# A graph tensor product on one core: the edges in four parts instead of three, and the sums' product with its operands exchanged

## The chip, the cores and the metric

The kernel runs on one core of a Trainium2 chip. The core has five engines with queues of their own: TensorE for matmuls (PE in the profile; PEld is its loading of weights), VectorE (DVE), ScalarE (ACT), GpSimd (POOL) and SyncE (SP), which here only issues transfers (DMAs). The metric is the device time of one execution in microseconds. Each engine works through its own queue in order; semaphores tie the queues together.

## The reference

The graph has N = 10000 nodes and E = 640000 edges with random ends. A node carries x of 64 channels by 4 components, an edge carries Y of 4 values and 4 features.

```python
R = _silu(edge_feat @ w_rad)                              # (E, C)
xs = x[src]                                                 # (E, C, M)
tp = jnp.einsum('eci,ef,ifo->eco', xs, Y, cg)             # (E, C, M)
msg = R[:, :, None] * tp
agg = _segment_sum(msg.reshape(-1, C * M), dst, N).reshape(N, C, M)
return jnp.einsum('ncm,cd->ndm', agg, w_mix)
```

All in float32. Since cg and w_mix don't depend on the edge, the kernel sums over edges first: for each node n it forms G[c, i, f] = sum over its edges of R[c] x[src][c, i] Y[f], 64 by 4 by 4 numbers, and multiplies that once by the product of w_mix and cg.

## The kernel before, in words

**Sorting by destination.** The sum over edges is a matmul with a one-hot matrix of destinations, so the edges have to lie together by destination. A bucket is 32 nodes (`NB`), 313 buckets in all; a group is 18 buckets (`B`), 18 groups, the last with 7 buckets. The edges, 128 to a column, make 5000 columns ("tiles"). They are cut into parts by `SPLIT`, each an entry of a share of the edges and the tiles that a bucket gets in this part, as a tuple of steps: `((0.26, (4,)), (0.47, (4, 4)), (0.27, (5,)))` is three parts, with one step of 4 tiles, two steps of 4, and one of 5. Together a bucket has 17 tiles (`BT`) of 128 places; what doesn't fit goes to an overflow area.

`pass1` sorts a part's edges into groups, `pass2` sorts a group of a part (a "segment") into buckets. Both work in chunks (12 and 11 tiles): places by small matmuls (`tables`, `places`), a one-hot matrix and the payload spread over rows (`spread`, DVE and ACT), a chain of matmuls that moves the rows (`move`, L560 and L562), an eviction on ACT (L567), and an indirect DMA on POOL that stores the rows in HBM (`store`, L571). `tables` (L319) is a chain of many small operations on PE, ACT and DVE, once for a block of pass 1 and once for a segment of pass 2; its first product is L333, its last L459. HBM areas for the rows of groups and of buckets are cleared first (`clear_groups`, L225; `clear_buckets`, L243).

**Messages.** `messages` walks the segments in order; a unit is one step of one bucket. For a unit, POOL gathers x of the sources (L785, one indirect DMA of 128 rows per tile), six units ahead, into eight buffers; PE transposes the payload (`turn`, L798), ACT copies it (L803), PE forms the radial product (`radial`, L808), ACT takes silu in place in PSUM (`silu`, L811), DVE multiplies x by it (`products`, L829) and builds S = onehot(dst) * Y, 128 columns of 32 nodes by 4 values, per tile (`spots`, L819 and L822). Then `sums` (L840) multiplies: for each tile and each half h of the 256 columns of V = R * x, V's half is the stationary operand and S streams past it, 128 moving columns:

```python
nc.tensor.matmul(G[:, h].rearrange("p n f -> p (n f)"),
                 V[:, t, 32 * h:32 * h + 32, :].rearrange("p c i -> p (c i)"),
                 S[:, t].rearrange("p n f -> p (n f)"), ...)
```

G lies in PSUM in one buffer, 128 channel-component rows of two halves by 128 columns. After the last step of a bucket in this part, `evict` takes it out: in the first part by an ACT copy (L871), later by a DVE add (L869) of the older sum, which `fetch` (L854) loads from HBM four units ahead. All but the last part store the sum in HBM again (`sums`, L873). In the last part the add writes Gs, four buckets side by side; `mix` (L888) multiplies Gs by the prepared weights with eight products of 256 moving columns, ACT copies the result (L896) and SP stores it.

**What sets the order.** The loop of `messages` runs over units, each in four quarters; the tuple `quarters` says which stage of which unit is emitted in which quarter (`(sums, 0)` the present unit, `(products, 1)` the next, `(gather, LG)` six on). PE, DVE and ACT run in the order in which this is written. `groups` puts steps of pass 2 of the next segment, and of pass 1 of the next part, between the quarters, evenly over the time there is. The first part's pass 1 has no messages beside it; only clearing is woven into it (`weave`). After the messages, `overflow` works through the rows that didn't fit, 128 edges in each trip of a loop.

Of the kernel before, what the change touches and what calls it, by code (L numbers as in the profile page):

```python
# [18 lines left out]
F = mybir.dt.float32  # L19
# [3 lines left out]
AF = mybir.ActivationFunctionType  # L23
AX = mybir.AxisListType

P = 128
B = 18
# [4 lines left out]
NB = 32  # L32
GN = B * NB
BT = 17
UT = 5
SPLIT = ((0.26, (4,)), (0.47, (4, 4)), (0.27, (5,)))
LG = 6
LI = 8
HEAVY = 4
# [32 lines left out]
class Kernel:  # L72
    def __init__(self, ctx, tc, x, src, dst, Y, ef, w_rad, cg, w_mix, out):
# [53 lines left out]
        self.p1.dst = self.dr.tile([self.p1.rows, self.p1.rw], F, name="grp")  # L127
        self.p2.dst = self.dr.tile([self.p2.rows, self.p2.rw], F, name="bkt")

        self.sums = self.dr.tile([self.NBK, P, 256], F, name="sums")  # L130
        self.in_group = {"grp": 0, "bkt": 0}
        self.tab = {}
        self.held, self.wanted, self.pos = None, False, None
# [607 lines left out]
    def messages(self):  # L741

        nc, ph = self.nc, self.ph
        units = [((k, g), j, s) for k, g in self.segs for j in range(self.nb(g)) for s in range(len(SPLIT[k][1]))]
        MT = max(sum(u) for _, u in SPLIT)
        n = len(units)
        IDX, XG, PRE, ST_, RT, SS, VS, GP, GS, OLD = ({} for _ in range(10))

        def quad(k):

# [80 lines left out]
        def sums(k):  # L831
            g, j, s = units[k]
            ut = tiles(k)[1]
            if s == 0:
                GP[g, j] = self.ps.tile([P, 2, NB, 4], F, name="G", tag="G", bufs=1)
            G = GP[g, j]
            V, S = VS.pop(k), SS.pop(k)
            for t in range(ut):
                for h in range(2):
                    nc.tensor.matmul(G[:, h].rearrange("p n f -> p (n f)"),  # L840
                                     V[:, t, 32 * h:32 * h + 32, :].rearrange("p c i -> p (c i)"),
                                     S[:, t].rearrange("p n f -> p (n f)"),
                                     start=(s + t + h == 0), stop=(last(k) and t == ut - 1),
                                     skip_group_check=True)

        def last(k):
            return units[k][2] == len(SPLIT[units[k][0][0]][1]) - 1

        def fetch(k):

            g, j, s = units[k]
            if g[0] and s == 0:
                OLD[g, j] = ph.tile([P, 2, 4, NB], F, name="old", bufs=4)
                nc.sync.dma_start(OLD[g, j].rearrange("p h f n -> p (h f n)"), self.sums[g[1] * B + j])  # L854

        def evict(k):
            g, j, s = units[k]
            if not last(k):
                return
            final = g[0] == len(SPLIT) - 1  # L860
            if not final:
                to = ph.tile([P, 2, 4, NB], F, name="Gp")
            else:
                if j % 4 == 0:
                    GS[g, j // 4] = ph.tile([P, 2, 4, 4, NB], F, name="Gs")
                to = GS[g, j // 4][:, :, :, j % 4, :]
            G = GP.pop((g, j)).rearrange("p h n f -> p h f n")
            if g[0]:
                nc.vector.tensor_tensor(to, OLD.pop((g, j)), G, op=OP.add)  # L869
            else:  # L870
                nc.scalar.activation(to, G, AF.Copy)  # L871
            if not final:
                nc.sync.dma_start(self.sums[g[1] * B + j], to.rearrange("p h f n -> p (h f n)"))  # L873

        def full(k):
            g, j, s = units[k]
# [15 lines left out]
        def mixed(k, po):  # L892
# [230 lines left out]
```

## Time and profile before

| | us |
|---|---|
| median of 3 runs | 10905.27 (10901.35 to 10920.43) |
| the profiled execution | 10989.96 |
| its span, first to last instruction | 10987.9 |
| first sums matmul (L840) starts | 726.6 |
| overflow loop and end, from | 10935 |

| engine | busy us | share | instructions |
|---|---|---|---|
| PE | 8420.1 | 77% | 52157 |
| PEld | 7126.3 | 65% | 52157 |
| DVE | 7056.8 | 64% | 13530 |
| ACT | 4102.8 | 37% | 12301 |
| POOL | 6003.7 | 55% | 6286 |

A float32 matmul stands as two records, each with its own weight load; a transpose is one. PE's busy time overlaps itself, since a record lasts longer than the distance to the next. In a row of a group, the numbers behind the bar are busy time, the mean of one in ns, and the idle time of the engine before these instructions with what ended it; "issue" is idle time for which no wait is seen. The mean granted clock of TensorE is 0.834. Units of the three parts begin at 727, 3678 and 8364 us.

### The profile page before, as it was taken

What the parts mean: (1) busy time and instruction counts of PE and PEld (TensorE: products, weight loads), DVE (VectorE), ACT (ScalarE), POOL (GpSimd) and SP (SyncE); (2) the same over time, 40 slices, a digit from 0 to 9 for tenths busy, and PEclk for the clock granted to TensorE, in tenths of its full rate; (3) what the DMA queues carried; (4) which work ended last, traced back from release to release, by engine and by line L of the source; (5) the groups of instructions that cost most, each with busy time, mean ns of one, the idle gap of its engine ahead of it and who ended that gap; (6) DMA issues with size and microseconds to landing.
All of it is one profiled execution on the core that took longest, in us unless ns stands there. A gap on an engine that the chain in (4) does not pass through costs nothing. (4 is left out here: it accounts for less than half of the span.)

```text
span 10987.9 us, 150963 instructions
## 1 busy us (share of the span) xinstructions
PE 8420.1 (77%) x52157; PEld 7126.3 (65%) x52157; DVE 7056.8 (64%) x13530; ACT 4102.8 (37%) x12301; POOL 6003.7 (55%) x6286
## 2 busy tenths in 40 slices
PE   6767787777877777777767777777767888888886
PEld 5656676666765666666656666666656666666665
DVE  7767777777766666666656666665546655656553
ACT  5645454554543433333333333333313222222220
POOL 1235455555555555555555556565566666666664
PEclk8878888888888888888888788888878888888887
DMA  7222222222223333333333333333333333333332
GB/s 155 77 62 80 83 84 86 83 82 85 87 84 93 96 99 98 99 98 99 99 94 97 92 95 102 98 103 97 96 110 103 106 107 107 104 104 107 107 103 86
DMA packets 695214, 1057.15 MB, mean 96 GB/s; under 512 B 251068, under 2 KB 499025, under 8 KB 694448
## 3 DMA queue, kind: packets, MB, share of 16 engines
q0 software_dynamic: 285872, 746.46, 23.6%
q1 hardware_dynamic: 405984, 294.29, 9.6%
q8 instruction: 413, 6.77, 0.3%
q10 hardware_dynamic: 2592, 6.74, 0.2%
q14 instruction: 353, 2.89, 0.1%
HBM read 856.14 MB, written 206.13 MB: 97 GB/s over the span
## 5 line engine op out<-in xcount | busy, mean ns | idle before, releaser
L785 POOL DMA_INDIRECT xg<-in_x_dram,sidx x5321 | 5052.2, 949 | 3344.1 <-issue 1371.8
L840 PE MATMUL G<-S,xg 128*128 128x128 f32 x21284 | 3250.8, 313 | 681.0 <-issue 395.4
L840 PEld LDWEIGHTS G<-S,xg 128*128 128x128 f32 x21284 | 3053.5, 226 | 797.3 <-issue 461.7
L560 PE MATMUL pr<-X,oh 128*128 128x126 f32 (+1 forms) x21252 | 3097.7, 306 | 604.6 <-ACT rt L567 294.1
L560 PEld LDWEIGHTS pr<-X,oh 128*128 128x128 f32 x21252 | 2929.4, 217 | 800.6 <-issue 384.2
L829 DVE TENSOR_TENSOR xg<-xg,pre 128x1024 f32<-128x1024 f32 (+1 forms) x1252 | 1603.8, 1281 | 866.8 <-ACT pre L811 705.8
L537 DVE TENSOR_TENSOR X<-dv,Wt 128x1485 f32<-128x1485 f32 (+3 forms) x941 | 1596.0, 1696 | 699.4 <-remote 413.2
L552 ACT ACTIVATE sq<-i,rowf 128x128 f32<-128x128 f32 x5640 | 1743.6, 393 | 5.6 <-DVE rowf L524 4.8
L811 ACT ACTIVATE pre<-pre 128x256 f32<-128x256 f32 (+1 forms) x1252 | 477.5, 381 | 2998.4 <-remote 990.0
L808 PE MATMUL pre<-wr,sT 36*128 36x256 f32 (+1 forms) x2504 | 1020.4, 490 | 310.1 <-ACT sT L803 256.4
L822 DVE TENSOR_TENSOR S<-dv,pay 128x512 f32<-128x512 f32 (+1 forms) x1252 | 907.6, 725 | 280.0 <-remote 131.0
L553 ACT ACTIVATE oh<-sq,ones 128x768 f32<-128x768 f32 (+1 forms) x941 | 928.5, 987 | 152.9 <-remote 50.9
L571 POOL DMA_INDIRECT grp<-rt,idx x417 | 415.2, 996 | 921.3 <-ACT rt L567 498.7
L571 POOL DMA_INDIRECT bkt<-rt,idx x524 | 524.8, 1002 | 646.6 <-ACT rt L567 422.0
L546 DVE TENSOR_TENSOR oh<-dv,rowf 128x768 f32<-128x768 f32 (+2 forms) x939 | 803.5, 856 | 0.3 <-PE pre L798 0.2
L808 PEld LDWEIGHTS pre<-wr,sT 36*128 36x128 f32 (+1 forms) x2504 | 414.6, 206 | 514.4 <-ACT sT L803 290.3
L567 ACT ACTIVATE rt<-pr 128x135 f32<-128x135 f32 (+1 forms) x941 | 253.6, 270 | 1075.9 <-remote 636.0
L869 DVE TENSOR_TENSOR Gs<-old,G 128x256 f32<-128x256 f32 x313 | 131.5, 420 | 766.5 <-PE G L840 277.9
L798 PE MATMUL pre<-ident,pay 128*36 128x128 f32 (+1 forms) x1252 | 383.2, 306 | 129.1 <-DVE xg L829 97.5
L798 PEld LDWEIGHTS pre<-ident,pay 128*36 128x36 f32 (+1 forms) x1252 | 132.7, 106 | 515.0 <-issue 235.5
L507 ACT ACTIVATE pc<-pp 128x432 f32<-128x432 f32 (+4 forms) x471 | 237.9, 505 | 559.7 <-remote 176.2
L803 ACT ACTIVATE sT<-pre 36x128 f32<-36x128 f32 (+1 forms) x1252 | 325.5, 260 | 285.6 <-PE pre L798 128.5
(214 smaller groups left out, 5164.6 us busy)
## 6 DMA issues: line engine op xcount, KB each, us to landing
xg<-in_x_dram,sidx POOLq DMA_INDIRECT x5321
sums<-Gp SPq DMA_DIRECT2D x626, 128.0 KB
old<-sums SPq DMA_DIRECT2D x626, 128.0 KB
bkt<-z SPq DMA_DIRECT2D x24, 994.5 KB
grp<-z SPq DMA_DIRECT2D x17, 679.5 KB
Wt<-grp SPq DMA_DIRECT2D x17, 679.5 KB
pay<-bkt SPq DMA_DIRECT2D x17, 648.0 KB
ys<-in_Y_dram SPq DMA_DIRECT2D x104, 96.0 KB
```

The lines of the kernel that those rows point to most:

```text
L537: nc.vector.tensor_tensor(X[:, :m, :].rearrange("p t (s w) -> p t s w", w=W), msk.unsqueeze(3).to_broadcast([P, m, ps.r, W]), QD[c // Q][1 ...
L546: nc.vector.tensor_tensor(oh[:, :v, :], self.v128.unsqueeze(1).to_broadcast([P, v, P]), row[:, o:o + v].unsqueeze(2).to_broadcast([P, v, P ...
L552: nc.scalar.activation(sq[:, u, :], self.i128, AF.Square, bias=to, scale=-1.0)
L553: nc.scalar.activation(oh[:, v:v + len(at), :], sq[:, :len(at), :], AF.Relu, bias=self.ones[:, 0:1], scale=-2.0)
L560: nc.tensor.matmul(pr[:, :ps.rw], oh[:, u, :], X[:, u, :], start=(u == 0), stop=(not on and u == m - 1))
L571: st = nc.gpsimd.indirect_dma_start(out=ps.dst, out_offset=bass.IndirectOffsetOnAxis(ap=idx[:, i:i + 1], axis=0), in_=RT.pop(c), in_offset ...
L785: nc.gpsimd.indirect_dma_start(out=xg[:, t, :], out_offset=None, in_=self.x, in_offset=bass.IndirectOffsetOnAxis(ap=si[:, u:u + 1], axis=0))
L798: nc.tensor.transpose(pre[:ut * W, 384:512], pb, self.ident)
L808: nc.tensor.matmul(R, ST_.pop(k)[:ut * W], self.wr[:ut * W, :ut * 64], start=True, stop=True)
L822: nc.vector.tensor_tensor(S[:, :ut], self.eq[:, :ut].unsqueeze(3).to_broadcast([P, ut, NB, 4]), pb[:, :, 1:5].unsqueeze(2).to_broadcast([P ...
L829: nc.vector.tensor_tensor(V, V, R.unsqueeze(3).to_broadcast([P, ut, 64, 4]), op=OP.mult)
L840: nc.tensor.matmul(G[:, h].rearrange("p n f -> p (n f)"), V[:, t, 32 * h:32 * h + 32, :].rearrange("p c i -> p (c i)"), S[:, t].rearrange( ...
```

## The change

There are four parts of one step each, with 3, 4, 5 and 5 tiles of a bucket; a bucket still has 17 tiles. In `sums`, S is the stationary operand and V streams past it with all its 256 columns, one matmul per tile; G then has the 128 node-value pairs as rows and the 256 channel-component pairs as columns. G and its transposed form take turns in the two halves of one PSUM bank. The sums in HBM keep their size, in the new orientation. In the last part the added sum stays in SBUF, two transposes per bucket (`flip`, a step later, behind the next unit's sums) bring it to the old orientation in the other half, and an ACT copy (`flipped`) writes it to Gs.

```diff
-SPLIT = ((0.26, (4,)), (0.47, (4, 4)), (0.27, (5,)))
+SPLIT = ((0.185, (3,)), (0.235, (4,)), (0.3, (5,)), (0.28, (5,)))
...
-        self.sums = self.dr.tile([self.NBK, P, 256], F, name="sums")
+        self.sums = self.dr.tile([self.NBK, NB * 4, 256], F, name="sums")
...
+        bank = self.ps.tile([P, 2, 256], F, name="G", tag="G", bufs=1)
+        turns = itertools.cycle((0, 1))
+        half = lambda: bank[:, next(turns), :]
...
-                GP[g, j] = self.ps.tile([P, 2, NB, 4], F, name="G", tag="G", bufs=1)
+                GP[g, j] = half()
...
-                for h in range(2):
-                    nc.tensor.matmul(G[:, h].rearrange("p n f -> p (n f)"),
-                                     V[:, t, 32 * h:32 * h + 32, :].rearrange("p c i -> p (c i)"),
-                                     S[:, t].rearrange("p n f -> p (n f)"),
-                                     start=(s + t + h == 0), stop=(last(k) and t == ut - 1),
-                                     skip_group_check=True)
+                nc.tensor.matmul(G, S[:, t].rearrange("p n f -> p (n f)"), V[:, t].rearrange("p c i -> p (c i)"),
+                                 start=(s + t == 0), stop=(last(k) and t == ut - 1), skip_group_check=True)
...
-            final = g[0] == len(SPLIT) - 1
...
+            to = ph.tile([P, 256], F, name="Gp")
+            G = GP.pop((g, j))
             if g[0]:
                 nc.vector.tensor_tensor(to, OLD.pop((g, j)), G, op=OP.add)
             else:
                 nc.scalar.activation(to, G, AF.Copy)
...
+            if g[0] < len(SPLIT) - 1:
+                nc.sync.dma_start(self.sums[g[1] * B + j], to)
+            else:
+                GE[k] = to
+
+        def flip(k):
+
+            if k not in GE:
+                return
+            Ge = GE.pop(k)
+            GT[k] = half()
+            for h in range(2):
+                nc.tensor.transpose(GT[k][:, h * P:(h + 1) * P], Ge[:, h * P:(h + 1) * P], self.ident)
+
+        def flipped(k):
+            g, j, s = units[k]
+            if k not in GT:
+                return
+            if j % 4 == 0:
+                GS[g, j // 4] = ph.tile([P, 2, 4, 4, NB], F, name="Gs")
+            nc.scalar.activation(GS[g, j // 4][:, :, :, j % 4, :],
+                                 GT.pop(k).rearrange("p (h n f) -> p h f n", h=2, f=4), AF.Copy)
...
-        quarters = (((index, LI), (gather, LG), (fetch, 4), (turn, 2), (sums, 0), (silu, 1)), ((turned, 2), (spots, 1)),
-                    ((products, 1), (evict, 0)), ((radial, 2), (full, -1)))
+        quarters = (((index, LI), (gather, LG), (fetch, 4), (turn, 2), (sums, 0), (flip, -1), (silu, 1)),
+                    ((turned, 2), (spots, 1)), ((products, 1), (evict, 0), (flipped, -1)), ((radial, 2), (full, -1)))
```

More of the change, by code (lines that the diff above doesn't have):

```diff
@@ L746, in messages @@
         n = len(units)
-        IDX, XG, PRE, ST_, RT, SS, VS, GP, GS, OLD = ({} for _ in range(10))
+        IDX, XG, PRE, ST_, RT, SS, VS, GP, GS, OLD, GE, GT = ({} for _ in range(12))
+        bank = self.ps.tile([P, 2, 256], F, name="G", tag="G", bufs=1)
+        turns = itertools.cycle((0, 1))
+        half = lambda: bank[:, next(turns), :]
         def quad(k):
@@ L852, in fetch @@
             if g[0] and s == 0:
-                OLD[g, j] = ph.tile([P, 2, 4, NB], F, name="old", bufs=4)
-                nc.sync.dma_start(OLD[g, j].rearrange("p h f n -> p (h f n)"), self.sums[g[1] * B + j])
+                OLD[g, j] = ph.tile([P, 256], F, name="old", bufs=4)
+                nc.sync.dma_start(OLD[g, j], self.sums[g[1] * B + j])
         def evict(k):
@@ L859, in evict @@
                 return
-            final = g[0] == len(SPLIT) - 1
[L861 to L867, printed above, removed]
+            to = ph.tile([P, 256], F, name="Gp")
+            G = GP.pop((g, j))
             if g[0]:
@@ L871, in evict @@
                 nc.scalar.activation(to, G, AF.Copy)
-            if not final:
-                nc.sync.dma_start(self.sums[g[1] * B + j], to.rearrange("p h f n -> p (h f n)"))
+            if g[0] < len(SPLIT) - 1:
[17 more added lines that the diff above has]
+                                 GT.pop(k).rearrange("p (h n f) -> p h f n", h=2, f=4), AF.Copy)
         def full(k):
```

## The prediction

> **What bounds the kernel now.** I read the page's totals first, then the span cut where the work changes: the opening (two of its stretches), the messages of part 0, 1 and 2, and the overflow loop. Columns: microseconds; busy time and instructions of PE, PEld, DVE, ACT, POOL; granted TensorE clock; DMA share; GB/s.
>
> ```profile
> PE 8420.1 (77%) x52157; PEld 7126.3 (65%) x52157; DVE 7056.8 (64%) x13530; ACT 4102.8 (37%) x12301; POOL 6003.7 (55%) x6286
> 203.00:455.00 252.00, 182.71 (x1296) 155.82 (x1296) 189.31 (x363) 153.79 (x463) 45.62 (x47) 0.82 0.30 103
> 568.00:727.00 159.00, 78.17 (x441) 61.68 (x442) 99.47 (x306) 63.60 (x184) 43.01 (x45) 0.66 0.18 47
> 727.00:3678.00 2951.00, 2325.62 (x15325) 2010.25 (x15323) 2133.80 (x4201) 1449.80 (x4374) 1534.67 (x1594) 0.86 0.29 86
> 3678.00:8364.00 4686.00, 3512.89 (x21378) 2979.15 (x21378) 2894.11 (x5319) 1575.10 (x4719) 2736.20 (x2863) 0.82 0.34 98
> 8364.00:10935.00 2571.00, 2086.19 (x12026) 1717.35 (x12025) 1491.17 (x2702) 656.98 (x1953) 1573.61 (x1654) 0.85 0.37 106
> 10935.00:10988.00 53.00, 14.37 (x46) 8.79 (x46) 14.03 (x63) 2.27 (x9) 7.81 (x8) 0.56 0.04 11
> ```
>
> A unit (the tiles of one bucket that are summed in one step) takes 2951/313 = 9.43 us in part 0, 4686/626 = 7.49 in part 1, 2571/313 = 8.21 in part 2. TensorE is busiest (79, 75, 81 per cent) and never full. The end of the messages shows how the engines hang together:
>
> ```profile
> 10546.00:10699.00 153.00, 122.94 (x719) 101.62 (x719) 88.59 (x161) 41.00 (x122) 93.05 (x98) 0.85 0.35 102
> 10699.00:10829.00 130.00, 95.69 (x494) 78.52 (x493) 51.43 (x73) 12.34 (x42) 83.27 (x89) 0.79 0.38 113
> 10908.00:10935.00 27.00, 25.87 (x170) 21.80 (x169) 15.30 (x23) 3.54 (x11) 0.43 (x1) 1.00 0.11 34
> ```
>
> The first two rows are 18 units each: 8.5 us a unit with sorting beside them, 7.2 without; where gathers have ended too (third row), PE is busy 96 per cent. So both the gather queue on POOL and the sort cost time. The groups of the gathers and of the changed product:
>
> ```profile
> L785 POOL DMA_INDIRECT xg<-in_x_dram,sidx x5321 | 5052.2, 949 | 3344.1 <-issue 1371.8 <-PE G L840 1068.8 <-remote 415.8
> L840 PE MATMUL G<-S,xg 128*128 128x128 f32 x21284 | 3250.8, 313 | 681.0 <-issue 395.4 <-DVE Gp L869 133.7 <-DVE Gs L869 81.8
> L840 PEld LDWEIGHTS G<-S,xg 128*128 128x128 f32 x21284 | 3053.5, 226 | 797.3 <-issue 461.7 <-DVE Gp L869 155.4 <-DVE Gs L869 95.2
> ```
>
> A gather holds POOL for 0.949 us plus 1371.8/5321 = 0.26 of issue, 1.21 in all. Then POOL waits 1068.8 us for sums that free a gather buffer; PE in turn waits for evictions. I read the loop as coupled: work added to PE, VectorE or POOL shows in part.
>
> **The product.** A tile has four records now (two halves, two passes each) of 128 moving columns, and two of 256 after it. The mixing product already runs 256 columns over 128x128 weights, next to sums, at full clock:
>
> ```profile
> 10928.91 3.62 PE L888 MATMUL po<-wf,Gs 128*128 128x256 f32 x16
> 10932.36 2.39 PE L840 MATMUL G<-S,xg 128*128 128x128 f32 x20
> L888 PE MATMUL po<-wf,Gs x1392: 379/379/794, 8405.7 to 10938.6; 128*128 128x256 f32 x159, 128*64 128x256 f32 x38, 128*80 128x256 f32 x2
> L840 PE MATMUL G<-S,xg x21284: 269/275/583, 726.6 to 10934.5; 128*128 128x128 f32 x199
> ```
>
> Start to start that is (3.62 - 0.379)/15 = 0.216 us against (2.39 - 0.275)/19 = 0.111: the two short ones cost 0.222, the long one 0.216. The weight loads that vanish (10642 of 0.226) lie beside matmuls. Saved: 10642 x 0.006 = 64 us at full clock, 77 at the mean 0.83. Half of the 395.4 us of "issue" gaps could go with half of the records (198 more). Bounds: 0 and -275; I take -50, near the streaming rows, since PE has idle time around it.
>
> The Trainium skill, Perfetto Trace Analysis, section "Identifying the Most-Contended Engine", says that busy time of matmuls misleads and that TensorE's headroom is to be judged by the busy share of weight loads. By that rule 65 per cent falls by 14 points and the change should gain; the rows above show the loads hidden, so I give it only the chance of a rival below.
>
> **The opening.** Part 0 falls from 1296 tile columns to 936, so 108 chunks of 12 become 78 (the shares in the code, rounded to 24). At the end of the first pass a chunk takes 3.1 us (POOL starts); but before that the clearing of later parts' groups alternates with the stores into the same tensor:
>
> ```profile
> 482.37 0.97 POOL L571 DMA_INDIRECT grp<-rt,idx  x1 [2.53 <-ACT rt L567]
> 485.52 0.97 POOL L571 DMA_INDIRECT grp<-rt,idx  x1 [2.18 <-ACT rt L567]
> L225 SPq DMA_DIRECT2D grp<-z x36: 332/343/552, 203.5 to 453.0; - x36
>   POOL grp L571: 164.0, 21
> ```
>
> 36 clears (18 groups of two parts) take 203.5 to 453.0, 6.9 us each, and POOL's stores waited for them 164.0 us. Four parts make 54. The 30 chunks less are worth up to 30 x 3.1 = 93; 18 more clears eat back up to 18 x 6.9 = 124. Bounds -93 and +31; I take -50, since they interleave with chunks that have to run anyway.
>
> The 30 chunks aren't gone: they move beside the messages. Stores of chunks in each stretch:
>
> ```profile
> 727.00:3678.00 2951.00, 343.94 (x344) 0.86 0.29 86
> 3678.00:8364.00 4686.00, 352.15 (x351) 0.82 0.34 98
> ```
>
> That is 1.10 and 0.56 chunks a unit; the units differ by 9.43 - 7.49 = 1.94 us, or 3.6 a chunk, with tables and half of the evictions in it. The floor is a store on POOL, 1.00 plus 0.26 of issue, 1.26. Taken 2.5, between them: 30 x 2.5 = +75 (38 to 108).
>
> **More, smaller segments.** 18 groups times four parts are 72 bucket passes for 54, and 32 blocks of the first pass for 30: 20 more tables of places. Group tiles go from 5626 to 5695 and bucket chunks from 524 to 541. A table alone in the opening:
>
> ```profile
> 618.72 1.79 PE L333 MATMUL cnt<-D,sel 128*64 128x198 bf16 x8 [2.99 <-DVE D L309]
> 632.55 0.19 PE L459 MATMUL ovp<-fl,onesb 128*128 128x8 bf16 x1
> ```
>
> 14 us uncovered, of which PE works about 5 (its rows between these). Among messages other work fills most: between 0 and 20 x 14 = 280; I take 3 each, under PE's own work, +60. The 17 chunks at 2 us are +34 (21 at POOL's floor to 61 at 3.6); they are emptier ones. SP's added loads, 18 of groups and 18 of payloads, run a segment ahead: hidden; if one weren't, it would cost the 14 us again.
>
> **Evictions and the sums in HBM.** Each bucket is now evicted four times for three; the added eviction is a VectorE add that also needs an old sum loaded and a new one stored.
>
> ```profile
> L871 ACT ACTIVATE Gp<-G 128x256 f32<-128x256 f32 x313 | 117.0, 374 | 312.3 <-PE G L840 164.7 <-remote 77.3 <-PE pre L798 24.2
> L869 DVE TENSOR_TENSOR Gp<-old,G 128x256 f32<-128x256 f32 x313 | 130.9, 418 | 439.6 <-remote 224.6 <-PE G L840 82.3 <-PE pre L798 70.9
> PE G L840 <- ACT Gp L871: 56.4, 25, 6.4
> sums<-Gp SPq DMA_DIRECT2D x626, 128.0 KB
> old<-sums SPq DMA_DIRECT2D x626, 128.0 KB
> ```
>
> VectorE gets 313 x 0.418 = 131 us, half hidden in its idle third. Behind the eviction stand the next bucket's first matmul, and behind that PE's whole queue and POOL's freed buffers. PE waited 133.7 us for 313 such adds; 313 more cost the like. After the change G alternates between halves of one PSUM bank. If the halves are guarded apart, all of it goes: 133.7 + 56.4 = -190; if by bank, nothing does and +134 comes. Bounds -190 and 134 + 131 = +265. I take +60 for add and wait: the wait partly replaces "issue" gaps. No run here has two halves of a bank in turn. The Trainium skill, PSUM — Partial Sum Buffer, section "PSUM bank collisions raise a hardware error", says that two engines on one bank and quadrant collide whichever columns they touch, two readers too, and should be guarded by bank; by that rule it is the +134 end, and the next part's ACT copy is ordered too.
>
> 313 more stores and loads of 128 KB are 80 MB, at 30 to 37 per cent DMA share and fetched four units (30 us) ahead: nothing. With that cover gone they cost 80 MB at 100 GB/s, 800 us, which I hold for excluded. SP's fetch waits for the eviction four units back, with stores and part loads behind it; those are due units later.
>
> **Turning the sums back.** Part 3 adds 626 transposes, 313 ACT copies and a wait of the next sums for that copy.
>
> ```profile
> L798 PE MATMUL pre<-ident,pay 128*36 128x128 f32 (+1 forms) x1252 | 383.2, 306 | 129.1 <-DVE xg L829 97.5
> ```
>
> Streamed they cost 626 x 0.111 = 69 us, alone 626 x 0.306 = 192. The copy is like L871, 313 x 0.374 = 117, on an ACT busy 26 per cent there; PE has radial, turn and sort work over it. Together +50 (0 to 309). The rest of a unit keeps its count, 1252, and its 17 tiles a bucket.
>
> **The tail.** Counting the drawn destinations against the rows a bucket holds leaves 14 rows of 15 over, two trips of the overflow loop; four parts leave 19, three trips.
>
> ```profile
> 10952.50 0.99 POOL L1001 DMA_INDIRECT oxg<-in_x_dram,osi  x1 [4.32 <-DVE odst L999]
> 10970.74 0.96 POOL L1001 DMA_INDIRECT oxg<-in_x_dram,osi  x1 [4.91 <-DVE odst L999]
> ```
>
> One trip is +18.
>
> **Sum.** -50 - 50 + 75 + 60 + 34 + 60 + 50 + 18 = +197 us. The profiled execution took 10989.96 (span 10987.9); 11187 by that. It lies 84.7 over the median of the three runs, 10905.27, so there I forecast 11102, 1.8 per cent slower. The bounds add to -481 and +1072; they won't all fall on one side.
>
> **Rivals.**
> - *The gather queue sets the pace.* In the 18 units without sorting POOL's 90 gathers take 90 x 1.21 = 109 of 130 us. Then PE and VectorE additions hide, and only POOL's count: (30 + 17) x 1.26 = 59, the tail 18, the opening -50: 10932, almost no change. Against it: POOL waits 1068.8 us for PE's sums.
> - *The weight loads do bind* (faster; the skill's rule above). Place: the sums on PE. It decides once a dropped load saves over 0.023 us: 10642 x 0.023 = 247, the other terms' sum. At a third of its 0.226, 0.075, the gain is 798 and the time 10905 + 247 - 798 = 10354; at 0.04, 10726. For it: issue gaps of 395.4 us sit before these records. Against: 0.111 to 0.216.
> - *The halves really alternate* (faster). PE's waits of 190 go in place of +60: 197 - 60 - 190 = -53, 10852.
> - *Turning back stalls part 3.* If each unit waits in full for copy and transposes, and for the eviction, +309 and +134 in place of 50 and 60: 11435. For it: VectorE's adds waited long already in part 2 (the 81.8 us and more of PE above). Against: ACT is idle three quarters there.
>
> **Numbers.** Forecast 0.50, POOL's pace 0.17, halves 0.12, loads 0.13, stall 0.08. About 0.2 per cent (22 us) is what a measurement here can tell from no change. Faster: halves and loads, a third of POOL's pace (an opening at -93) and 0.02 of the forecast: 0.32. Same: half of POOL's pace, 0.08. Slower 0.60. The range 10760 to 11340 cuts deep gains of the loads and the worst of the stall; the likeliest case alone is 10990 to 11300.
>
> **What would show it.** Sums: 10642 records near 0.38 us, spaced 0.216; spaced under 0.2, or fewer issue gaps, speak for the loads. First gather 40 to 60 us earlier, 54 clears. Units near 6.7, 8.4, 9.6 and 8.6 us in the four parts, 33.3 a bucket (now 10208/313 = 32.6); POOL's pace would keep it at 32.8. PE's waits for Gp near 270 us, or near none if halves alternate. Three trips at the end. Wrong it is if the units add up to no more than 10208 us.

## The result and the profile after

The changed kernel takes 11232.12 us (median of 4 runs, 11211.35 to 11259.7) against 10904.12 for the kernel before on the same chip: a ratio of 1.0293, with a 95 per cent interval of 1.0275 to 1.0312. It is slower by 328 us; the forecast was 11102, slower by 197. Its profiled execution took 11236.54 us, 4 over its median, where that of before lay 86 over. So the two traces differ by 247 us only, and a stretch compared between them shows some 80 us too little.

The totals of the page after, then a cut into windows: the four parts of the messages and the overflow loop. Columns as in the prediction.

```profile
PE 8437.2 (75%) x42637; PEld 6598.1 (59%) x42637; DVE 7400.0 (66%) x15220; ACT 4272.3 (38%) x12860; POOL 6050.1 (54%) x6307
```

```profile
669.00:2763.00 2094.00, 1636.86 (x8748) 1287.85 (x8748) 1516.38 (x3420) 1014.80 (x3148) 1116.34 (x1158) 0.84 0.33 93
2763.00:5376.00 2613.00, 2014.77 (x10415) 1590.77 (x10415) 1901.63 (x3948) 1051.98 (x3170) 1454.60 (x1510) 0.84 0.38 108
5376.00:8421.00 3045.00, 2279.04 (x11258) 1781.40 (x11258) 2052.50 (x3901) 1101.98 (x3248) 1758.04 (x1829) 0.82 0.38 106
8421.00:11161.00 2740.00, 2132.89 (x9689) 1624.09 (x9689) 1513.71 (x2795) 794.97 (x2374) 1598.15 (x1674) 0.84 0.35 99
11161.00:11235.00 74.00, 20.48 (x64) 12.26 (x62) 20.90 (x92) 4.00 (x15) 10.85 (x11) 0.56 0.04 12
```

A unit takes 6.69, 8.35, 9.73 and 8.75 us in the four parts (a window over 313). In the traces the opening is shorter by 57 us (726.6 to 669.1), the messages longer by 284 and the tail by 21. TensorE's busy time has stayed where it was, with 9,500 records fewer. VectorE's has grown by 343 us; that is more than the 131 us of the added sums.

The groups of the product and of its sums, after:

```profile
L844 PE MATMUL G<-xg,S 128*128 128x256 f32 x10642 | 3060.1, 438 | 371.4 <-issue 172.0 <-DVE Gp L864 84.2 <-ACT Gs L887 63.6
L844 PEld LDWEIGHTS G<-xg,S 128*128 128x128 f32 x10642 | 2247.0, 222 | 793.8 <-issue 210.9 <-DVE Gp L864 112.1 <-ACT Gs L887 74.6
L864 DVE TENSOR_TENSOR Gp<-old,G 128x256 f32<-128x256 f32 x939 | 392.3, 418 | 1091.7 <-remote 470.5 <-PE G L879 312.6 <-PE G L844 170.4
L879 PE MATMUL G<-ident,Gp 128*128 128x128 f32 x626 | 132.8, 292 | 19.0 <-issue 17.6 <-ACT Gs L887 1.0
L887 ACT ACTIVATE Gs<-G 128x256 f32<-128x256 f32 x313 | 118.9, 380 | 809.6 <-DVE Gp L864 602.5 <-issue 132.5 <-DVE xg L834 73.9
```

The product itself is no dearer: TensorE waits 371 us ahead of it, where it waited 681. Two groups of waits have grown. One is in the opening (the views of waits and of the line's instructions, after):

```profile
POOL grp L571 <- DMA grp<-z: 241.3, 31, 79.2
PE cnt L333 <- DVE D L309: 200.7, 21, 101.8
```

```profile
L225 SPq DMA_DIRECT2D grp<-z x54: 332/343/1027, 212.8 to 535.3; - x54
```

```profile
450.00:500.00 50.00, 0.00 (x0) 0.00 (x0) 0.00 (x0) 0.00 (x0) 9.83 (x11) 0.50 0.19 73
```

The last of the 54 clears is issued at 535. PE, VectorE and ACT have run out of work by 450 and wait for the last stores of the first pass, which alternate with clears.

The other lies in `tables`, which works out the places of a segment. The waits of PE that name its small VectorE operations, before and after:

```profile
PE cnt L333 <- DVE D L309: 117.0, 24, 31.3
PE stp L417 <- DVE bs L405: 104.7, 37, 7.3
PE ovp L457 <- DVE fl L452: 31.1, 28, 2.4
PE ddp L435 <- DVE to L429: 49.8, 36, 4.4
```

```profile
PE stp L417 <- DVE bs L405: 139.9, 40, 8.6
PE ovp L457 <- DVE fl L452: 79.5, 40, 3.4
PE ddp L435 <- DVE to L429: 71.2, 52, 8.6
PE stp L417 <- DVE dl L398: 65.5, 18, 5.3
```

Summed over all groups of the lines of `tables`, PE stood 614.3 us ahead of them before and 920.5 after: 306 more, of which 84 are the longer wait for D in the opening (117.0 before). The other 222 are 11 us for each of the 20 added tables. They aren't all lost: PE's idle time as a whole (span less busy time) has grown by 230 us only, since ahead of the sums it is 310 shorter. The chain of one table, from the timeline after, in part 3 (start, duration, operation, and in brackets the idle time before it):

```profile
8990.51 0.80 PE L813 MATMUL pre<-wr,sT 45*128 45x320 f32 x2
8995.81 0.32 PE L417 MATMUL stp<-bs,onesb 9*128 9x171 bf16 x1 [4.50 <-DVE dl L398]
8996.06 0.44 PE L803 MATMUL pre<-ident,pay 128*45 128x128 f32 x1
8996.30 3.55 PE L844 MATMUL G<-xg,S 128*128 128x256 f32 x10
...
9000.73 0.55 PE L435 MATMUL ddp<-bd,ones 9*128 9x171 f32 x2 [0.49 <-DVE to L429]
9004.66 0.17 PE L457 MATMUL ovp<-fl,Ub 128*128 128x9 bf16 x1 [3.38 <-DVE fl L452]
```

```profile
8991.14 0.17 DVE L317 CAST f<-ri 64x18 f32<-64x18 int32 x1
8991.34 0.17 DVE L368 SCALAR_TENSOR_TENSOR part<-f,pre 64x18 f32<-64x18 f32 x1
...
8995.02 0.17 DVE L398 TENSOR_TENSOR dl<-dl,st 9x18 f32<-9x18 f32 x1
...
8995.44 0.32 DVE L405 TENSOR_TENSOR bs<-ident,st 9x171 bf16<-9x171 f32 x1
...
9000.96 1.48 DVE L834 TENSOR_TENSOR xg<-xg,pre 128x1280 f32<-128x1280 f32 x1
9002.35 0.42 DVE L864 TENSOR_TENSOR Gp<-old,G 128x256 f32<-128x256 f32 x1
```

From 8991 to 8996 VectorE works through some 25 operations, mostly of 0.17 us and mostly on the result of the one before. PE's next instruction is the table's small matmul that needs their end, so PE stands for 4.5 us; the payload's transpose and ten records of sums that follow it in PE's order come after. PE stands again at 9001, for 3.4 us. Here VectorE's order has its part: a product (L834) and an add (L864) of the messages come first, 1.8 us in all, and only then the table's steps that PE waits for.

### The profile page after: what moved, and what is told of

It is laid out like the page before. It is cut to its first block, busy times and chain, and to the rows that moved or that the text cites. A ratio compares the mean times of both kernels' runs of the same rounds, so it can differ in the third digit from the quotient of the medians.

```text
span 11234.8 us, 135460 instructions
## 1 busy us (share of the span) xinstructions
PE 8437.2 (75%) x42637; PEld 6598.1 (59%) x42637; DVE 7400.0 (66%) x15220; ACT 4272.3 (38%) x12860; POOL 6050.1 (54%) x6307
## 5 line engine op out<-in xcount | busy, mean ns | idle before, releaser
L790 POOL DMA_INDIRECT xg<-in_x_dram,sidx x5321 | 5075.2, 954 | 3413.0 <-issue 1373.5
L560 PE MATMUL pr<-X,oh 128*128 128x135 f32 (+1 forms) x21390 | 3143.9, 308 | 693.6 <-ACT rt L567 317.4
L844 PE MATMUL G<-xg,S 128*128 128x256 f32 x10642 | 3060.1, 438 | 371.4 <-issue 172.0
L844 PEld LDWEIGHTS G<-xg,S 128*128 128x128 f32 x10642 | 2247.0, 222 | 793.8 <-issue 210.9
L834 DVE TENSOR_TENSOR xg<-xg,pre 128x1280 f32<-128x1280 f32 (+2 forms) x1252 | 1603.6, 1281 | 1033.0 <-ACT pre L816 724.3
L816 ACT ACTIVATE pre<-pre 128x320 f32<-128x320 f32 (+2 forms) x1252 | 478.8, 382 | 2238.5 <-remote 727.2
L813 PE MATMUL pre<-wr,sT 45*128 45x320 f32 (+2 forms) x2504 | 1005.1, 484 | 272.7 <-ACT sT L808 183.6
L864 DVE TENSOR_TENSOR Gp<-old,G 128x256 f32<-128x256 f32 x939 | 392.3, 418 | 1091.7 <-remote 470.5
L553 ACT ACTIVATE oh<-sq,ones 128x768 f32<-128x768 f32 (+2 forms) x958 | 939.6, 981 | 174.5 <-remote 55.2
L827 DVE TENSOR_TENSOR S<-dv,pay 128x640 f32<-128x640 f32 (+2 forms) x1252 | 907.1, 725 | 135.1 <-PE G L844 41.7
L546 DVE TENSOR_TENSOR oh<-dv,rowf 128x640 f32<-128x640 f32 (+3 forms) x939 | 805.4, 858 | 1.2 <-remote 0.8
L813 PEld LDWEIGHTS pre<-wr,sT 45*128 45x128 f32 (+2 forms) x2504 | 411.1, 205 | 547.2 <-issue 245.7
```

What stands on the lines that cost most here:

```text
L546: nc.vector.tensor_tensor(oh[:, :v, :], self.v128.unsqueeze(1).to_broadcast([P, v, P]), row[:, o:o + v].unsqueeze(2).to_broadcast([P, v, P ...
L553: nc.scalar.activation(oh[:, v:v + len(at), :], sq[:, :len(at), :], AF.Relu, bias=self.ones[:, 0:1], scale=-2.0)
L560: nc.tensor.matmul(pr[:, :ps.rw], oh[:, u, :], X[:, u, :], start=(u == 0), stop=(not on and u == m - 1))
L790: nc.gpsimd.indirect_dma_start(out=xg[:, t, :], out_offset=None, in_=self.x, in_offset=bass.IndirectOffsetOnAxis(ap=si[:, u:u + 1], axis=0))
L813: nc.tensor.matmul(R, ST_.pop(k)[:ut * W], self.wr[:ut * W, :ut * 64], start=True, stop=True)
L827: nc.vector.tensor_tensor(S[:, :ut], self.eq[:, :ut].unsqueeze(3).to_broadcast([P, ut, NB, 4]), pb[:, :, 1:5].unsqueeze(2).to_broadcast([P ...
```

## The experiments

The runs came from four chips. On the first two the kernel before takes 10904 and 10970 us, on the other two 8900 and 8895, with the same kernel and the same durations of nearly all instructions (more on that at the end). So each run is compared by its ratio to the kernel before on its own chip.

**The split alone.** The kernel before with the new shares and the old product.

```diff
-SPLIT = ((0.26, (4,)), (0.47, (4, 4)), (0.27, (5,)))
+SPLIT = ((0.185, (3,)), (0.235, (4,)), (0.3, (5,)), (0.28, (5,)))
```

> The kernel before with the four parts alone, the old product and no turning back. Theory (the split costs by its added segments, chunks and evictions, the product gives next to nothing): the opening ends about 55 us earlier, the tail has a third trip (+20), the messages take 200 to 250 us more; about +190 us over the kernel before, 11095. Rival (turning back stalls part 3 and makes most of the loss): no more than +60 us here.

Measured: ratio 1.0371 (1.0354 to 1.0388), 398 us over the 10970 of that chip. The split alone is dearer than the whole change and about twice what I gave it.

**The product alone.** The changed kernel with the old shares.

```diff
-SPLIT = ((0.185, (3,)), (0.235, (4,)), (0.3, (5,)), (0.28, (5,)))
+SPLIT = ((0.26, (4,)), (0.47, (4, 4)), (0.27, (5,)))
```

> The changed kernel with the old three parts: the exchanged operands and the turning back alone. Theory: the saved record overhead (50 us) and the turning back (50 to 100) nearly cancel; 0 to +80 us over the kernel before, nearly all of it in the last part. Rival (weight loads bind): 200 us or more under the kernel before, in all three parts. Rival (turning back stalls the last part): +200 us or more, in the last part.

Measured: ratio 1.0059 (1.0042 to 1.0076), 65 us slower. Halving the number of weight loads, with the turning back that it needs, gains nothing by itself here. I had expected the loss in the last part, and the trace doesn't show it there: 8.26 us a unit, against 8.21 on the first chip, which is 0.6 per cent faster. On top of the new split the same exchange is worth 1.0371 less 1.029 to 1.031, a gain of some 0.6 to 0.8 per cent. The units get shorter in parts that carry sorting (6.86 to 6.69 us in part 0, 9.85 to 9.73 in part 2, on chips that differ by 0.6 per cent) and not in the last part, which turns back (8.75 in both). Why the exchange loses with three parts and gains with four isn't shown; these differences are little more than two executions of one kernel can differ by (86 us over 1252 units is 0.07).

**No turning back.** The changed kernel, where VectorE's last add writes Gs in place of the transposes and the ACT copy.

```diff
+            if final:
+                if j % 4 == 0:
+                    GS[g, j // 4] = ph.tile([P, 2, 4, 4, NB], F, name="Gs")
+                to = GS[g, j // 4][:, :, :, j % 4, :]
+                G = G.rearrange("p (h n f) -> p h f n", h=2, f=4)
+                old = OLD.pop((g, j)).rearrange("p (h n f) -> p h f n", h=2, f=4)
+                nc.vector.tensor_tensor(to, old, G, op=OP.add)
+                return
...
-        quarters = (((index, LI), (gather, LG), (fetch, 4), (turn, 2), (sums, 0), (flip, -1), (silu, 1)),
-                    ((turned, 2), (spots, 1)), ((products, 1), (evict, 0), (flipped, -1)), ((radial, 2), (full, -1)))
+        quarters = (((index, LI), (gather, LG), (fetch, 4), (turn, 2), (sums, 0), (silu, 1)),
+                    ((turned, 2), (spots, 1)), ((products, 1), (evict, 0)), ((radial, 2), (full, -1)))
```

> The changed kernel without the two transposes and the copy of each bucket in the last part; the add writes Gs at once, so the mixing product gets the sums in the wrong orientation and the output isn't the reference's. Theory: the fourth part falls from 8.75 us a unit to 8.45, 60 to 120 us in all, and the other parts stay. Rival (the stall makes the loss): 250 us or more.

Measured: ratio 1.040 (1.0373 to 1.0427), above the changed kernel's 1.029 to 1.031 on other chips. The last part takes 8.93 us a unit, where the changed kernel took 8.75; the other parts differ by no more than 1.1 per cent (6.76, 8.42 and 9.78). One group of the last part became slower (instructions of that line in this run):

```profile
L869 DVE TENSOR_TENSOR Gs<-old,G x313: 592/606/645, 8486.1 to 11275.9; 128x256 f32<-128x256 f32 x157
```

The add that writes in strides takes 0.606 us instead of 0.418, 59 us more on VectorE between a bucket's sums and the next. The edit thus changes two things: it says that turning back costs less than this slower add does, and no more. How much of the transposes (133 us of PE's busy time) and the copies (119 of ACT's) is hidden isn't shown by itself.

**The clears first, before.** The kernel before, with the clears of later groups issued beside the first 40 steps of the first pass.

```diff
-                for _ in range(40):
-                    next(first, None)
-                later = itertools.chain(self.clear_buckets(),
-                                        *(self.clear_groups(k, nc.sync) for k in range(1, len(SPLIT))))
-                run(weave(first, later, 0.75))
+                groups = itertools.chain(*(self.clear_groups(k, nc.sync) for k in range(1, len(SPLIT))))
+                run(weave(itertools.islice(first, 40), groups, 0.9))
+                run(weave(first, self.clear_buckets(), 0.75))
```

> The kernel before, where the clearing of the later parts' groups is put among the first 40 steps of the opening, before most stores, and the clearing of buckets after it. Theory (a group clear that alternates with stores holds the opening 6.9 us): the first sums start 60 to 120 us earlier than 726.6 and the whole is as much faster, about 10815. Rival (the transfers themselves bind the opening, in whatever order): under 20 us.

Measured: ratio 0.9984 (0.9973 to 0.9996), 18 us by the ratio (25 between the medians); the first sums start at 722.2. The alternation of clears and stores cost the kernel before nearly nothing; something else holds its first pass, and what it is wasn't tried.

**The changed kernel again**, on the chip of the next runs.

> The changed kernel as it stands, once more beside the kernel before, to have its units on the chip of the runs that price work. Theory (the split costs, the product gives a little back, turning back is hidden): ratio 1.029 within 0.003; units 6.7, 8.4, 9.75 and 8.75 us in the four parts. Rival (the first ratio belonged to its chip; turning back is what the run without it saved): ratio near 1.040 or above, part 3 at 8.9 us a unit or more.

Measured: 9177.36 against 8899.55, ratio 1.031 (1.0293 to 1.0327), 278 us. Units of 5.72, 6.89, 7.63 and 6.83 us: all shorter than on the first chip, and the price of the change in proportion is the same.

**Work that nobody waits for.** Three loads on the kernel before: a VectorE add per unit, four more transposes per unit, a gather per unit.

```diff
+            nc.vector.tensor_tensor(self.spare, self.i128.unsqueeze(1).to_broadcast([P, 2, P]),
+                                    self.i128.unsqueeze(1).to_broadcast([P, 2, P]), op=OP.add)
```

```diff
+            for _ in range(5):
+                nc.tensor.transpose(pre[:ut * W, 384:512], pb, self.ident)
```

```diff
+            spare = ph.tile([P, 256], F, name="spare", bufs=1)
+            nc.gpsimd.indirect_dma_start(
+                out=spare, out_offset=None, in_=self.x,
+                in_offset=bass.IndirectOffsetOnAxis(ap=si[:, t0:t0 + 1], axis=0))
```

> The kernel before with one added VectorE add of 128x256 float32 into a spare tile behind each of the 1252 products (nothing reads it, the output is unchanged): 1252 x 0.42 = 526 us of VectorE work that frees nothing and that nothing waits for, except what is queued behind it. Theory of the coupled loop: a third to half of it shows, +175 to +265 us (ratio 1.016 to 1.024). Rival, the gather queue sets the pace: at most +40 us (1.004). Rival, VectorE's order is the path: all of it, +450 us or more (1.041).

> The kernel before with each unit's transpose of the payload done five times in place of once (same result each time): 5008 more TensorE records of 128 columns, streamed 0.111 us each, 556 us of PE work. Theory of the coupled loop: a third to half shows, +185 to +280 us (ratio 1.017 to 1.026). Rival, the gather queue sets the pace: at most +40 us. Rival, PE's order is the path: +500 us or more (1.046).

> The kernel before with one added gather of 128 rows per unit into a spare tile that nothing reads (the output is unchanged): 1252 x 1.21 = 1515 us of POOL work and 164 MB more from HBM. Theory of the coupled loop: half to four fifths shows, +750 to +1210 us (ratio 1.07 to 1.11). Rival, the gather queue sets the pace: all of it or more, +1500 us (1.138). Rival, PE and VectorE set the pace and POOL has room: under +300 us (1.028).

Measured: ratios 1.0108 (1.0091 to 1.0125), 1.0073 (1.0056 to 1.009) and 1.2385 (1.2365 to 1.2406): +94, +64 and +2121 us. The groups of the added work, in the first and in the third of these runs:

```profile
L831 DVE TENSOR_TENSOR spare<-i 128x256 f32<-128x256 f32 x1252 | 523.9, 418 | 0.0
```

```profile
L785 POOL DMA_INDIRECT xg<-in_x_dram,sidx x5321 | 5048.9, 949 | 1678.7 <-issue 1470.7 <-PE G L844 35.9 <-DVE didx L772 28.8
L789 POOL DMA_INDIRECT spare<-in_x_dram,sidx x1252 | 1192.5, 953 | 1254.1 <-DMA spare<-in_x_dram,sidx 820.4 <-issue 200.7 <-DVE xg L833 88.9
```

VectorE's 524 us show as 94 (18 per cent) and PE's 556 as 64 (12). With the added transposes the mean granted clock is 0.921, where it is 0.90 in the kernel before, so part of PE's work may be paid by that. The gathers show nearly in full: my edit also made them wait for their forerunner's landing in the one spare tile, 820 us in all, and if all of that is lost time, 2121 - 820 = 1301 us are left of the 1515 expected. With them POOL hardly waits for sums any more (35.9 us, 295 and 317 in the other two runs). So on this chip the gather queue sets the pace of streaming work, and the "third to half" that I had for PE and VectorE is too much. This is my first rival's mechanism, and yet the change costs 3 per cent on this chip too. The 343 us that it adds to VectorE would at 18 per cent cost some 62 (an estimate from these runs), so most of the price isn't streaming work.

**One more eviction per bucket, and no segment more.** The kernel before, where part 1 evicts after each of its two units.

```diff
-            if s == 0:
-                GP[g, j] = self.ps.tile([P, 2, NB, 4], F, name="G", tag="G", bufs=1)
-            G = GP[g, j]
+            G = GP[g, j] = self.ps.tile([P, 2, NB, 4], F, name="G", tag="G", bufs=1)
...
-            if g[0] and s == 0:
+            if g[0]:
...
             if not last(k):
-                return
+                to = ph.tile([P, 2, 4, NB], F, name="Gp")
+                G = GP.pop((g, j)).rearrange("p h n f -> p h f n")
+                nc.vector.tensor_tensor(to, OLD.pop((g, j, s)), G, op=OP.add)
+                MID[g, j] = to
+                nc.sync.dma_start(self.spare[g[1] * B + j], to.rearrange("p h f n -> p (h f n)"))
                 return
...
-                nc.vector.tensor_tensor(to, OLD.pop((g, j)), G, op=OP.add)
+                old = OLD.pop((g, j, s))
+                nc.vector.tensor_tensor(to, MID.pop((g, j), old), G, op=OP.add)
```

> The kernel before, three parts, in which part 1 evicts its sums after each of its two units instead of after both: 313 more VectorE adds, 313 more loads of an old sum and 313 more stores (to a second tensor that nobody reads), as the fourth part brings them, and not one segment, table or chunk more. Theory A (the round trip of the sums is what made the split dearer than forecast): +130 to +265 us, ratio 1.012 to 1.024. Theory B (the smaller segments made it dearer): the eviction is worth what the forecast gave it, +60 give or take 40, ratio 1.002 to 1.009. If 80 MB more of traffic were uncovered: +800 us.

**Every table twice.** The kernel before, where each bucket pass works out its places into scratch first.

```diff
+            nc.vector.tensor_copy(self.kx[:, :B], kc)
+            nc.vector.tensor_copy(self.kx[:, B:], self.kov[:, 1:2])
+            yield from self.tables(ps, D, nt, self.kx[:, :B], self.kx[:, B:], base, self.bc)
             yield from self.tables(ps, D, nt, kc, self.kov[:, 1:2], base, self.bc)
...
-        return (self.gt[k][g] + 23) // 24 + 12 +
+        return (self.gt[k][g] + 23) // 24 + 24 +
```

> The kernel before, in which each of the 54 bucket passes works out its table of places twice (first into scratch, then as before) and is given the steps for it in its plan. Theory B (segments dearer than forecast): 10 to 14 us a table, +540 to +756 us, ratio 1.05 to 1.07. Theory A, and the forecast: 3 us a table, +162 us, ratio 1.015. If the tables lie in idle time: under +40 us.

Measured, on one chip: the evictions 1.004 (1.0027 to 1.0052), +40 us; the tables 1.0678 (1.066 to 1.0696), +603 us, which is 603/54 = 11.2 us a table. Both lie where the second theory had them: an added eviction costs less than forecast, a table in the mean nearly four times as much. (In the run with evictions the second unit's add reads the first unit's sum, and the added load of an old sum isn't read: an add that waits for its load would not show there.) The waits of PE and ACT ahead of a table's steps, in the run with evictions and in that with tables twice:

```profile
PE stp L418 <- DVE bs L406: 188.7, 67, 5.1
PE ovp L458 <- DVE fl L453: 40.7, 37, 2.7
ACT ov L464 <- PE ovp L460: 182.9, 74, 6.2
```

```profile
PE stp L418 <- DVE bs L406: 501.4, 117, 14.8
PE ovp L458 <- DVE fl L453: 201.6, 89, 3.2
ACT ov L464 <- PE ovp L460: 657.2, 125, 12.1
```

Over all its lines PE stands 545 us ahead of table steps in the first and 1070 in the second, 9.7 more for each added table. VectorE's added work is (7586.4 - 7049.6)/54 = 9.9 us a table, against the run with more transposes, which leaves VectorE's work as it was (totals of the two pages; tables twice first):

```profile
PE 7901.0 (83%) x53437; PEld 6749.0 (71%) x53437; DVE 7586.4 (80%) x16392; ACT 4180.1 (44%) x12625; POOL 6020.3 (63%) x6286
```

```profile
PE 7920.1 (88%) x57165; PEld 6841.5 (76%) x57165; DVE 7049.6 (79%) x13530; ACT 4180.5 (47%) x12301; POOL 6012.5 (67%) x6286
```

But PE's standing isn't the price. Ahead of the sums it stands less when the tables are doubled (evictions first, then tables twice):

```profile
L839 PE MATMUL G<-S,xg 128*128 128x128 f32 x21284 | 2877.2, 294 | 407.3 <-DVE Gp L874 239.7 <-DVE Gs L874 120.2 <-DVE Gp L860 39.2
L844 PE MATMUL G<-S,xg 128*128 128x128 f32 x21284 | 3003.6, 303 | 15.8 <-DVE Gp L873 8.8 <-DVE Gs L873 3.0 <-ACT Gp L875 1.2
```

The two traces are 558 us apart. PE's idle time grew by 176 of them, its busy time by 381: 186 for the tables' own records, the rest because records of other lines last longer, the sums above among them, at a mean granted clock of 0.878 for 0.898. Nor is the price the same everywhere. Between the first sums of the parts in these two traces, the 3 added tables in the opening make 32 us, 17 in part 0 make 242, 19 in part 1 make 39 (some 79 without the other run's added evictions, which are all there), and 15 in part 2 make 246: 11, 14, 2 to 4, and 16 us a table. PE's added standing ahead of tables is 31, 105, 238 and 150 us in the same four stretches. Part 1 is the one where a segment has 36 units and not 18; whether that is the reason wasn't tried.

Still the two experiments with VectorE work make a pair: 524 us that nobody waits for cost 94, 537 us in chains that PE waits for in order cost 603. The tables bring PE work too, but more of that, in loose transposes, cost only 64.

**The clears first, after.** The same edit of the clears on the changed kernel.

> The changed kernel with the clears of all later groups issued beside the first 40 steps of the first pass, and the clears of the buckets after them, so that they no longer alternate with stores to the end of the pass. Theory (in the changed kernel the opening waits for its 54 clears: PE, VectorE and ACT idle from 445 to 540 us): first sums at about 570 us instead of 669, the kernel some 90 us faster than the changed one, ratio to the kernel before 1.021. Rival (the opening waits for its chunks and tables, as in the kernel before, where the same edit gave 25 us): 0 to 25 us, ratio 1.027 to 1.029.

Measured: ratio 1.0242 (1.0225 to 1.0259) against 1.031 without it: a gain of 0.7 per cent, some 60 us. First sums and clears (the views of the two lines):

```profile
L225 SPq DMA_DIRECT2D grp<-z x54: 332/722/1387, 23.3 to 80.3; - x54
```

```profile
L844 PE MATMUL G<-xg,S x10642: 379/379/797, 564.3 to 9028.6; 128*128 128x256 f32 x198
```

The sums start at 564, where the changed kernel on a like chip starts them at 636. The last clear is issued at 80 us instead of 519. So the clears did hold the opening of the changed kernel; the theory held, at two thirds of the size.

**A smaller first part, without a fourth.** The kernel before with the clears first and other shares.

```diff
-SPLIT = ((0.26, (4,)), (0.47, (4, 4)), (0.27, (5,)))
+SPLIT = ((0.24, (4,)), (0.48, (4, 4)), (0.28, (5,)))
```

> The kernel before with its three parts and its product, but shares of 0.24, 0.48 and 0.28 for 0.26, 0.47 and 0.27 (tiles 4, 8 and 5 as before), and the clears of the groups first as in the run above. About 8 chunks fewer in the opening, 8 x 3.1 = 25 us, and 25 us from the clears; the chunks come back beside messages at 2.5 us each, +20, and a trip more or less at the end is 18. Theory: 0 to 50 us faster, ratio 0.995 to 1.000. Rival (fuller rows in part 0 mean more trips at the end): up to 20 us slower, ratio 1.002.

Measured: ratio 0.9964 (0.995 to 0.9979), 8864.97 against 8894.98, 30 us. It is faster than both kernels: the sums start at 641.9, earlier than in the kernels with the old shares on such chips (702.6 with the added evictions), and no segment and no table is added. Against that it has 16 more bucket chunks (540 for 524) and a third trip at the end. It differs from the kernel before in clears and shares at once, and the clears alone were worth 18 to 25 us on another chip; the shares' own part isn't measured.

## Why the prediction was right or wrong

The direction was right, and the time inside the range; 11102 was 130 us short. The units came out near the forecast's 6.7, 8.4, 9.6 and 8.6 us. The mechanism behind it was half right: the fourth part costs more than it brings, but in good part through its tables, which I held to be mostly hidden. That the sum still came near is partly luck, since smaller errors the other way made up for half of that one. The terms, on the chips where they could be taken apart (the change there: +278 us):

| step | forecast | measured |
|---|---|---|
| opening | -50 | -67 (703, as in the runs with loads or evictions added, to 636) |
| 20 more tables | +60 | 20 x 603/54 = +223, at the mean price |
| evictions and the round trip | +60 | +40 |
| product and turning back | -50 + 50 | -52 (278 less 0.0371 x 8900 = 330 for the split alone) |
| tail | +18 | +20 |
| 30 chunks moved, 17 more | +75 + 34 | +114, what is left |
| sum | +197 | +278 |

The chunks aren't measured by themselves: they are the remainder, 2.4 us a chunk, near the 2.5 and 2 taken. The term for the product mixes two kinds of chips, and the two added tables of the first pass are priced like those of the bucket passes. The tables' term is the mean price of doubled tables, carried over. At the 14 and 16 us of parts 0 and 2, whose segments have 18 units like nearly all of the changed kernel's, it would be an estimated 284 to 328, and only 53 to 9 would be left for the chunks: how the two share 337 us stays open.

- *The product.* Right in its mechanism: ten records in a row, after, take 2.32 us, (2.32 - 0.379)/9 = 0.216 each, as the mixing product had shown, and the weight loads were hidden.

```profile
10392.75 2.32 PE L844 MATMUL G<-xg,S 128*128 128x256 f32 x10
```

- *The loads bind* (rival). Wrong: PEld's busy time fell by 528 us, its share from 65 to 59 per cent (I had taken 14 points), and the product alone made the kernel slower. The Trainium skill (Perfetto Trace Analysis, "Identifying the Most-Contended Engine") judges TensorE's headroom by the matmul work it does against its peak and by the weight loads' busy share. That fewer loads must then gain time was my own inference from it, and it doesn't hold here.
- *The halves.* As taken: they don't alternate. In the trace after, no first matmul of a bucket starts before the eviction of the bucket before it has ended; the closest follows by 0.05 us in parts 0 to 2. In part 3 the ACT copy is ordered behind the next bucket's add, 602.5 us of ACT's waits; that they cost little is likely, as the last part takes 8.75 us a unit with the split alone too, but wasn't tested apart. The Trainium skill (PSUM — Partial Sum Buffer, "PSUM bank collisions raise a hardware error") says to guard by bank and quadrant, or simply by bank; these waits agree with a guard by bank. But the wait that I expected from it, near 270 us, is 84.2 + 31.1 + 63.6 = 179: the "+134 end" for waits was no end, since PE arrives later anyway.
- *The opening.* Right in size, wrong in the reason for its bound: I had seen that 54 clears could eat the gain, and they did eat some 60 to 70 us that the opening could have given besides, but I took the alternation for a cost in the kernel before as well, where removing it gave 18 to 25.
- *More, smaller segments.* The step that failed. "14 us uncovered, of which PE works about 5 ... Among messages other work fills most ... I take 3 each, under PE's own work". A doubled table cost 11.2 us among messages, in the mean; the uncovered 14 us were nearer. I had other work fill the time, but PE's order is fixed: in the timeline it stands at a table's matmul until VectorE delivers, and the messages' matmuls that could fill the time are behind it. That this is why a table is dear is argued from the timeline; the standing and the price don't agree part by part, so what else is in the 11.2 us stays open. Moved to the forecast, 20 x 8.17 = 163 us is twice its shortfall of 81 on these chips; the product gives 52 back, the evictions 20 and the opening 17.
- *The gather queue sets the pace* (rival, 0.17). For streaming work it does, on the chip where I tested it; on the first chip, where the gathers leave POOL 1000 us of waits for sums, it wasn't tested. It didn't make the change cheap. A likely reason is that a chain stops the sums that POOL's buffers wait for: on the chip of the loads POOL waits 546 us for them in the changed kernel, 295 and 317 in the kernel before with loads on VectorE and PE.
- *Turning back stalls part 3* (rival). No: 8.75 us a unit for the 8.6 forecast, and 8.75 with the split alone, which turns nothing back.
- *The tail.* Three trips, +21 us.

That a table's matmuls would cost less if PE's order put them later (after the unit's sums that stand behind them) is what the timeline suggests, but it wasn't tried.

## What to carry to other kernels

Price a step by whether somebody in a fixed order waits for it, not by its engine's busy time: some 0.5 ms of VectorE work cost 94 us as loose adds and 603 us as tables, chains with PE and ACT steps between. A stretch where a chain runs uncovered shows its length (14 us here); inside an in-order stream it kept 14 to 16 us in two parts and 2 to 4 in another, so take the uncovered length for a start and measure. Before cutting work into more parts, count what each part repeats (here a table of 11 us in the mean per segment), and look whether other shares of the same parts give the gain without it.

## What the runs showed of the hardware

The same kernel takes 10.9 to 11.0 ms on two chips and 8.9 on two others. Single instructions are alike: a gather holds POOL for 954 ns in the changed kernel on the first chip and 952 on the other (5075.2/5321 and 5064.4/5321). What differs are waits. Those that the profile calls "remote" (it finds no instruction that ends when the signal comes) are among the longest on the first chip, 663 of them in the trace after, and there are none on the other. After, and the same kernel on the other chip, waits of ACT ahead of the same instruction:

```profile
ACT pre L816 <- remote: 727.2, 99, 16.7
ACT pre L816 <- PE pre L813: 534.2, 306, 13.9
```

```profile
ACT pre L816 <- PE pre L813: 1016.9, 609, 8.2
```

In the changed kernel 10335 records of TensorE (matmuls and weight loads) update one semaphore. The first chip's trace holds 8492 of these updates, the other's 10333. On the first chip the next update after an instruction's modelled end comes 0.01 us later (median) while POOL issues no DMAs, 0.45 us when POOL has issued them for 4 to 6 us with no gap over 1 us, and 2.4 us at 8 to 10; on the other chip it is 0.01 throughout. So signals come late there, or some of their records are missing and the next one is another's; the trace doesn't tell these apart. The mean granted clock is 0.83 on the first and 0.89 on the other. It need not be a cause: on the faster chips too it is 0.826 where PE is busy 72 per cent (gathers added), 0.898 at 84 (evictions added) and 0.921 at 88 (transposes added). Whether late signals alone make the 2 ms, and why one chip has them, stays open. The change costs 2.9 per cent on the first chip and 3.1 on the other.
